# A two-layer decode step on one core: the loads of K and V regrouped, the held matrices chosen one by one, and the steps between the layers rewritten

## The chip, the cores and the metric

The kernel runs on one core of a Trainium2 chip. The metric is the device time of one execution in microseconds; the median of several executions is compared. The core has five instruction streams: TensorE (PE: matrix multiplications, with the weight loads shown apart as PEld), VectorE (DVE), ScalarE (ACT), GpSimd (POOL) and SyncE (SP), which here does little but issue transfers from device memory to on-chip memory. ACT issues some transfers too. The streams wait for each other through semaphores. The transfers themselves are carried out by 16 DMA engines.

## The reference: what is computed

Four sequences (tokens 0 to 3), each with one new vector `x` of 448 numbers, pass twice through the same attention block and the same feed-forward block. The second pass uses the same weights and the same K and V as the first, so each matrix is wanted twice.

```python
W = min(4096, max(256, Sk // 4))                     # Sk = 8192, so 2048 keys
q = (x @ wq) in 16 heads of 256
k = repeat(k_cache[:, :, Sk - W:, :], 2)             # 8 KV heads, two query heads each
v = repeat(v_cache[:, :, Sk - W:, :], 2)
o = softmax(q k^T / 16) v
attention(x) = o @ wo                                # wq 448 x 4096, wo 4096 x 448
ffn(x) = (silu(x @ w_gate) * (x @ w_up)) @ w_down    # 448 x 1792, 448 x 1792, 1792 x 448

x = x + attention(layernorm(x));  x = x + ffn(layernorm(x))    # first layer
x = x + attention(layernorm(x));  x = x + ffn(layernorm(x))    # second layer, same arguments
```

All arguments are bfloat16. For one token and one KV head, K and V are 2048 x 256 numbers each, 1 MB each. There are 4 x 8 such pairs, and each is wanted in both layers: 64 MB of K and 64 MB of V if nothing were kept (MB is 1,048,576 bytes when a matrix is meant; in sums of traffic it is a million bytes).

## The kernel before

**Names.** A matrix is written as token, layer, KV head: `K204` is the K of token 2, KV head 4, read for its first layer (0); `V2130` is the first half of the V of token 2, head 3, in its second layer (1).

**Memory.** On chip there are 27 slots of half a megabyte (`half`, `NPOOL` = 27), 4 KB on each of 128 partitions. A K or V takes two. `wq` has a place of its own, as large as seven slots. `wo`, the gate, up and down weights have theirs. Each weight is read once.

**What is kept.** The last `KEEP_K[t]` K and `KEEP_V[t]` V of token t in its first layer stay in their slots until the second layer (line 36): 21 K and 18 V in all, always whole matrices. The others are read again.

**Order of the work.** `PLAN` (line 39) lists 44 stages. A stage has one or two batches, a batch one or two pairs of K and V (`+` or `&` joins two). First come mostly token 0's first layer, then token 1's first layer with token 0's second between it, and so on. The order of every engine's operations is written out by hand: `SEQ_PE`, `SEQ_DVE`, `SEQ_ACT`, `SEQ_POOL`, `SEQ_SP` hold the numbers of the operations in the order in which `build` makes them; in `SEQ_PE` a `w` is a filler, a 128 x 512 multiplication by zeros (line 1274) that keeps TensorE busy. `SLOTS` says which slot each load takes, in SP's order. `schedule` (line 230) adds the waits: a load into a slot waits until the PE instruction that last reads the slot's old content has run. Of the first loads, those before the first that must wait for a slot, every second one is issued by ACT instead of SP. All engines work strictly through their lists, so a load that waits holds back all loads behind it on SP.

**One batch** (`group`, line 816). The loads of K (line 829 whole: one transfer of 1 MB, 8 KB in one run on each partition; line 835 in halves: 4 KB runs, which skip the other half's 4 KB) and of V (line 851, always in halves: 8 keys, 4 KB, on each partition). DVE transposes each half of K in place (841). PE computes the scores (874), DVE the maximum (890), PE spreads it over the partitions (895, 898), DVE negates it (904), ACT takes the exponential (908), PE turns the weights round (921), ACT copies them out (930), PE sums them (938), DVE finishes the sums (943), PE multiplies with V (952), POOL inverts the sums (965), ACT and DVE fold the result (968, 970), PE flips it (976), DVE scales it (1006), and PE applies `wo` (1018 as columns, 1026 as rows). The scores release the slots of K, the product with V those of V. In the last stage the product with V is formed the other way round, V as the stationary operand (989).

**Between the layers.** When a token's eight heads are done, `rows` (760) brings the rows that line 1026 summed in PSUM back into a column: ACT copies them as bfloat16 (761), DVE takes the remainder (763), PE turns both (771), DVE adds (775). `residual` (778), then `norm` (530): DVE forms the weighted sum and the sum of squares (534, 537), PE spreads them (540), DVE subtracts the mean (544) and copies the two sums (546), PE and DVE prepare the last 64 of the 448 inputs (548, 551), POOL forms the inverse deviation in three steps (556, 558, 560). Then the feed-forward block, of two kinds. `ffn` (689; for tokens 0 and 3, whose weights are stationary, 56 multiplications for gate, 56 for up) works in columns: lines 720, 731, 734, 738, 748, 756. `ffn_row` (634; tokens 1 and 2, `ROWF`) works in rows 512 wide: lines 656, 662, 664, 666, 672, 684, and needs `rows` again at its end. After it come `norm` again and `qproj` (577): two strips 512 wide (594), two copies (600), two turns (610), a copy (617), a selection (625) and a copy (630). Tokens that have ended their second layer wait for the next token's feed-forward block and go through it together with that token.

**The end.** `finale` (1057) runs the last feed-forward block in columns (1117, 1128, 1149, 1152, 1157), turns all four results into rows (1172), adds the down projection in two strips of 224 (1182), copies (1188) and stores two halves of 4 x 224 (1190).

Of the kernel before, what the change touches and what calls it, by code (L numbers as in the profile page):

```python
# [5 lines left out]
ACT = mybir.ActivationFunctionType  # L6
# [7 lines left out]
B = 4  # L14
# [21 lines left out]
KEEP_K = (5, 5, 4, 7)  # L36
KEEP_V = (6, 5, 4, 3)
ROWF = (1, 2)
# [5 lines left out]
)  # L44
WHOLE = (
    "000 002 003 004 005 006 007 010 011 100 101 102 107 114 115 200 202 206"
)
SEQ_PE = (
# [294 lines left out]
def build(nc, A_x, A_k_cache, A_v_cache, A_wq, A_wo, B_x, B_w_gate, B_w_up, B_w_down, out):  # L343
# [3 lines left out]
    with ExitStack() as es:  # L347
# [58 lines left out]
        Ab = ps("A")  # L406
        Zb, Z2 = ps("Z"), ps("Z2")
        Av = Ab[:, 448:464].rearrange("p (c t) -> p c t", t=B)


        def c_ident0(e):
            e.memset(onesb[:, :], 1.0)
# [928 lines left out]
```

## Time and profile before

| | |
|---|---|
| median of 3 executions | 287.29 us (287.08 to 287.34) |
| span of the profiled execution | 290.4 us |
| busy: PE / DVE / POOL / ACT | 251.9 / 192.0 / 82.8 / 62.9 us |
| of PE's time, fillers (339) | 102.1 us |
| read from device memory | 105.48 MB |
| median time from issue to landing: V half / K half / K whole | 7.8 / 7.3 / 13.5 us |

The profiled execution is a single one and 3.1 us longer than the median. Engine times are sums over instructions that may overlap with those of other engines. In the tables of stretches, "DMA share" is the mean busy share of the 16 DMA engines (a little over 1 is possible, since packets overlap) and the last column what they moved.

### The profile page before, as it was taken

The numbers are of one execution on the slowest core, as the hardware profiler recorded it, in microseconds if no ns is written. First come the engines' busy times: TensorE is split into PE (matmuls) and PEld (weight loads), VectorE is DVE, ScalarE is ACT, GpSimd is POOL, SyncE is SP. The second block draws the span as 40 slices with busy tenths as digits, with TensorE's granted clock in tenths as the row PEclk, the third lists the DMA queues.
The fourth block names the chain that finished last, engine by engine and source line by source line (L and its number), as shares of the span: only waits on it lengthen the run. The fifth ranks groups of instructions, "written<-read, shape, count | busy, mean of one in ns | idle before, by whom it ended". The sixth has DMA issues, their size and how long they took to land.

```text
span 290.4 us, 11178 instructions
## 1 busy us (share of the span) xinstructions
PE 251.9 (87%) x4933; PEld 141.6 (49%) x4933; DVE 192.0 (66%) x594; ACT 62.9 (22%) x178; POOL 82.8 (29%) x233
## 2 busy tenths in 40 slices
PE   3989799899898999798989898988869988879976
PEld 1434344544474454354544544454536546745675
DVE  5527756547353895887867479959697679556532
ACT  0012011121202132213223122313323231223400
POOL 0071003031024224122423231605233162245231
PEclk9999889999999999999899999999999999999957
DMA  7999999999997999999999999999999999999800
GB/s 278 420 423 417 406 415 396 402 408 403 391 402 235 368 408 416 413 414 401 349 320 407 383 418 407 408 410 374 381 387 373 415 405 353 332 342 395 350 5 0
DMA packets 29192, 106.20 MB, mean 366 GB/s; under 512 B 2900, under 2 KB 7000, under 8 KB 26840
## 3 DMA queue, kind: packets, MB, share of 16 engines
q1 hardware_dynamic: 27424, 96.12, 85.3%
q10 hardware_dynamic: 1720, 9.37, 7.9%
q8 instruction: 38, 0.62, 0.9%
q14 instruction: 10, 0.08, 0.1%
HBM read 105.48 MB, written 0.00 MB: 363 GB/s over the span
## 4 chain that ended last, share of the span: by engine, by line
PE 42%; DMA 34%; DVE 16%; issue 2%; ACT 2%; SPq 2%; POOL 1%; DVEq 0%; ACTq 0%
DMA half<-in_A_k_cache_dram 29%; PE A L1274 13%; DVE half L841 10%; PE S L874 7%; PE Y L952 6%; DMA half<-in_A_v_cache_dram 5%; PE A L1026 2%; PE Z L720 2%; DVE oh L970 2%; PE Y L921 2%; PE Z L748 1%; ACT oh L968 1%; PE A L1018 1%; DVE tiny L890 1%; SPq L851 1%
## 5 line engine op out<-in xcount | busy, mean ns | idle before, releaser
L841 DVE STREAM_TRANSPOSE half<-half 128x1024 uint32<-128x1024 uint32 x86 | 105.4, 1233 | 12.2 <-DMA half<-in_A_k_cache_dram 12.1
L1274 PE MATMUL A<-identb,small 128*128 128x512 bf16 x339 | 102.1, 401 | 5.3 <-DVE A L434 4.8
L965 POOL TENSOR_TENSOR small<-small 128x2 f32<-128x2 f32 (+1 forms) x50 | 39.2, 789 | 57.3 <-DVE small L943 55.4
L952 PE MATMUL Y<-half,pT 128*4 128x256 bf16 (+1 forms) x992 | 43.3, 272 | 6.3 <-DMA half<-in_A_v_cache_dram 3.7
L874 PE MATMUL S<-half,qe 128*8 128x128 bf16 (+1 forms) x1600 | 41.6, 236 | 6.7 <-DVE half L841 2.3
L1274 PEld LDWEIGHTS A<-identb,small 128*128 128x128 bf16 x339 | 29.4, 104 | 33.1 <-issue 12.0
L874 PEld LDWEIGHTS S<-half,qe 128*8 128x8 bf16 x1600 | 28.9, 85 | 18.8 <-DVE half L841 4.5
L908 ACT ACTIVATE praw<-S,small 104x128 bf16<-104x128 f32 (+1 forms) x50 | 19.8, 397 | 82.2 <-DVE small L904 73.7
L880 POOL TENSOR_TENSOR qe<-qc,tiny 128x64 bf16<-128x64 bf16 x64 | 17.9, 293 | 51.1 <-PE S L874 37.5
L970 DVE SCALAR_TENSOR_TENSOR oh<-oh,small,Y 128x256 bf16<-128x256 bf16 x49 | 23.1, 472 | 13.4 <-ACT oh L968 12.9
L968 ACT ACTIVATE oh<-Y 128x256 bf16<-128x256 f32 x49 | 18.7, 382 | 49.0 <-PE Y L952 43.6
L952 PEld LDWEIGHTS Y<-half,pT 128*4 128x4 bf16 (+1 forms) x992 | 18.4, 83 | 17.8 <-DMA half<-in_A_v_cache_dram 5.4
L890 DVE TENSOR_REDUCE tiny<-S 104x1 bf16<-104x128 f32 (+1 forms) x50 | 15.9, 318 | 6.0 <-PE S L874 5.9
L930 ACT ACTIVATE pT<-Y 128x64 bf16<-128x64 f32 (+1 forms) x50 | 12.6, 252 | 33.0 <-PE Y L921 28.5
L1026 PE MATMUL A<-wo_sb,oT 128*4 128x448 bf16 x200 | 16.7, 352 | 1.8 <-DVE oT L1006 1.7
L556 POOL TENSOR_SCALAR st<-st 128x1 f32<-128x1 f32 x15 | 4.0, 265 | 48.0 <-DVE st L546 47.9
L904 DVE TENSOR_REDUCE small<-S 104x1 f32<-104x32 f32 x50 | 8.8, 179 | 11.8 <-PE S L898 11.4
L1212 POOL MEMSET oT<- 128x16 bf16 x40 | 4.1, 112 | 40.1 <-PE A L1026 30.5
L943 DVE TENSOR_REDUCE small<-Y 128x2 f32<-128x32 f32 (+1 forms) x50 | 9.3, 188 | 8.8 <-PE Y L938 8.5
L1006 DVE TENSOR_TENSOR oT<-Y,small 128x4 bf16<-128x4 f32 (+1 forms) x63 | 8.9, 154 | 6.8 <-PE Y L976 5.3
L976 PEld LDWEIGHTS Y<-tiny,oh 128*128 128x128 bf16 x98 | 6.7, 100 | 10.9 <-DVE oh L970 6.0
L976 PE MATMUL Y<-tiny,oh 128*128 128x2 bf16 (+1 forms) x98 | 9.7, 168 | 2.5 <-DVE oh L970 2.1
(181 smaller groups left out, 272.5 us busy)
## 6 DMA issues: line engine op xcount, KB each, us to landing
half<-in_A_v_cache_dram SPq DMA_DIRECT2D x90, 512.0 KB, 7.8
half<-in_A_k_cache_dram SPq DMA_DIRECT2D x55, 512.0 KB, 7.3
half<-in_A_k_cache_dram SPq DMA_DIRECT2D x10, 1024.0 KB, 13.5
half<-in_A_k_cache_dram ACTq DMA_DIRECT2D x5, 1024.0 KB, 23.4
wo_sb<-in_A_wo_dram SPq DMA_DIRECT2D x7, 448.0 KB, 16.0
wq_sb<-in_A_wq_dram ACTq DMA_DIRECT2D x2, 1024.0 KB, 8.8
wd_sb<-in_B_w_down_dram SPq DMA_DIRECT2D x1, 1568.0 KB, 15.6
wg_sb<-in_B_w_gate_dram SPq DMA_DIRECT2D x1, 1344.0 KB, 9.1
```

The lines of the kernel that those rows point to most:

```text
L841: return e.transpose(a, a)
L874: last = e.matmul(Sb[s_][qd:qd + 8, 0:32 * 2 * J], lhsT=qe[q_][:, P, ce, :, :].rearrange("p a n -> p (a n)"), rhs=keys(kcs[P], J * x, J, c ...
L880: g.op(POOL, "qe", lambda e, P=P, t=t, kvh=kvh: e.tensor_tensor(qe[q_][:, P, :, :, :], qc[t][:, kvh, :, :].unsqueeze(2).broadcast_to([128, ...
L890: g.op(DVE, f"max{n}", lambda e: e.tensor_reduce(pmax[s_][0:R, :], Sb[s_][0:R, 0:N], AX.X, ALU.max), r=(f"s{s_}",), w=(f"pmax{s_}",), bank ...
L908: return e.activation(praw[0:R, 0:128 * n].rearrange("p (g r l) -> p g r l", g=2 * n, l=2), Sb[s_][0:R, 0:128 * n].rearrange("p (l g r) -> ...
L952: last = e.matmul(Yb[p_][32 * gg:32 * gg + M, 256:512], lhsT=pT[pt][:, gg, 2 * a + hv, 4 * P:4 * P + M] if n == 2 else p1[:, gg % 2, 2 * a ...
L965: g.op(POOL, f"pow{n}", lambda e: e.tensor_tensor(ri[p_][:, 0:2 * n], rs[p_][:, 0:2 * n], expo[:, 1:1 + 2 * n], op=ALU.pow), r=(f"rs{p_}", ...
L968: g.op(SCA, "oh", lambda e: e.activation(oh[:, :], Yb[p_][:, 256:512], ACT.Copy), r=(f"y{p_}",), w=("oh",), bank=(f"Y{p_}",))
L970: g.op(DVE, "oho", lambda e: e.scalar_tensor_tensor(out=oh[:, :], in0=oh[:, :], scalar=lomask[:, 0:1], in1=Yb[p_][:, 256:512], op0=ALU.mul ...
L976: last = e.matmul(Yb[p_][:, 2 * n * dh:2 * n * dh + 2 * n], lhsT=oh[:, :].rearrange("p (m e) -> p e m", e=2)[:, dh, :], rhs=osel[:, 0:2 * ...
L1026: last = e.matmul(Ab[32 * k:32 * k + B, 0:D], lhsT=oT[oi][:, k % 2, k // 2, :], rhs=wo_sb[:, 4 * kvh + k, :], start=False, stop=False, ski ...
L1274: return e.matmul(Ab[:, 0:512], lhsT=zero[:, 0:1].broadcast_to([128, 128]), rhs=identb[:, :].unsqueeze(1).broadcast_to([128, 4, 128]), sta ...
```

## The change

The plan of the 44 stages, the slots (27), and what is computed stay. What changes:

- **Loads of K and V.** V is split like K, 16 keys in one run on each partition. 27 K (before 15) and 28 V (before none) are read as one transfer of 1 MB with 8 KB runs; 34 halves of K (56) and 39 halves of V (92) remain. Counted from `PLAN`, the lists of held and of whole matrices, K and V together need 91.5 MB of 1,048,576 bytes, before 89.
- **Held matrices.** `KEEP_K` and `KEEP_V` name them: the same K but for that of token 3, head 6 (20); 33 halves of V instead of 36 (four halves are no longer kept, one is new).
- **Slots.** `wq` lies behind the 27 slots in the same tensor. Its seven slots are used for loads after the last use of `wq` (the last q projection).
- **Orders.** `SEQ_*` and `SLOTS` are new. There are 201 fillers instead of 339: before the sixth stage's scores 8 instead of 125; in the last five stages 13, before none. At the start, loads of K and V stand before `x` and between the parts of `wq`.
- **`norm`**: the sum comes as a by-product of the residual's addition, POOL has one step (`power`) instead of three and a scaling; two small DVE steps are new.
- **`rows`**: one copy as float32 and a turn with float32 weights, no remainder.
- **Feed-forward block**: gate and up for all tokens as row strips of 256, 29 multiplications each; then 128 x 256 steps on ACT and DVE, two turns, a copy, the down projection in columns.
- **Softmax weights**: the exponentials stay in plain column order; the turn takes 16 or 32 small multiplications instead of 8.
- **q**: one strip of 256 (64 multiplications in four groups), one copy, 32 small turns, one copy.
- **The end**: gate and up as strips, down in four strips of 112; two finished tokens are stored earlier, two stages before the end, the other two at the end, each token by one transfer.

```diff
-KEEP_K = (5, 5, 4, 7)
-KEEP_V = (6, 5, 4, 3)
-ROWF = (1, 2)
+KEEP_K = (
+    "03 06 01 04 07 16 14 15 13 17 23 27 26 25 33 37 31 34 35 30"
+)
+KEEP_V = (
+    "030 031 060 061 010 011 050 051 040 041 070 071 160 161 140 141 150 151 130 170 171 230 270 271 260 261 251 331 "
+    "370 310 311 340 341"
+)
+EARLY = 2
...
+        held = [None] * npool + [late] * 7
...
-        wq_sb = sb("wq_sb", [128, 3 * 4096 + 2048], BF16)
-        kv = sb("half", [128, NPOOL * HALF], BF16)
+        kv = sb("half", [128, (NPOOL + 7) * HALF], BF16)
+        wq_sb = kv[:, NPOOL * HALF:(NPOOL + 7) * HALF]
...
-                    vsrc = A_v_cache[t, kvh, s0:s0 + WIN, :].rearrange("(a q g) d -> a q (g d)", a=2, q=128)
...
+                    vsrc = A_v_cache[t, kvh, s0:s0 + WIN, :].rearrange("(p j) d -> p (j d)", p=128)
+                    whole = f"{t}{layer}{kvh}" in WHOLE_V.split()
+                    if whole:
+                        g.dma(1 << 20, lambda e, vs=vs, vsrc=vsrc: e.dma_start(
+                            kv[:, HALF * vs[0][0]:HALF * vs[0][0] + 2 * HALF], vsrc[:, :]), None,
+                            w=tuple(f"v{t}_{kvh}_{hv}" for hv in range(2)), cells=tuple(vs), run=8192)
...
+        def power(dst, key, src, n):
+            g.op(POOL, f"pr{n}", lambda e: e.tensor_tensor(dst, src[:, 0:n], expo[:, 0:n], op=ALU.pow),
+                 r=("mixf" if src is mixf else "mixq", "expo"), w=(key,))
...
+                            for c, b, o, m in parts:
+                                last = e.matmul(zb[32 * j:32 * j + 8, o:o + m], lhsT=win(b, i, 8), rhs=w[:, c:c + m],
+                                                start=(cc == 0 and i == 0), stop=False, skip_group_check=True)
...
+            g.op(SCA, "rowcp", lambda e: e.activation(wide[:, 0:D], Ab[:, 0:D], ACT.Copy), r=(f"row{t}",), w=WIDE + ("wt", "wx", "wy"), bank=("A",))
...
+                    last = e.matmul(Zb[0:m, cc:cc + 1], lhsT=wide[:, 128 * cc:128 * cc + m], rhs=nmk[:, t, 0:1],
+                                    start=False, stop=False, skip_group_check=True)
```

More of the change, by code (lines that the diff above doesn't have):

```diff
@@ L228, in _count, with schedule @@
         o.dval = self.dcount[sem]
-    def schedule(self, npool, filler):
+    def schedule(self, npool, filler, lastq):
         real = len(self.ops)
@@ L248, in schedule @@
         last = {id(c): o for o in self.ops[:real] for c in o.rel}
-        held = [None] * npool
+        late = []
+        last[id(late)] = lastq
+        held = [None] * npool + [late] * 7
         slots = iter(SLOTS.split())
@@ L278, in schedule @@
                 o.start, o.pos = t, at[e]
-                o.end = free[e] = t + DUR[o.kind]
+                o.end = free[e] = t + DUR.get(o.kind, .3)
                 if o.nbytes:
@@ L370, in build @@
-        ri = [small[:, 14 + 2 * NS + 4 * (NY + i):18 + 2 * NS + 4 * (NY + i)] for i in range(NY)]
-        fars = small[:, 11:14].bitcast(BF16)
+        tiny = sb("tiny", [128, 12 + NS], BF16)
+        onesb, qmask, osel = tiny[:, 0:1], tiny[:, 2:6], tiny[:, 6:10]
+        par = tiny[:, 10:12]
+        pmax = [tiny[:, 12 + s:13 + s] for s in range(NS)]
+        sel2 = sb("sel2", [128, 4, 2, 12], BF16)
+        sel1 = sb("sel1", [128, 4, 4, 2, 2], BF16)
+        small = sb("small", [128, 32 + 2 * NS + 8 * NY], FP32)
@@ new lines, in build @@
+        inv, lomask, expo = small[:, 0:1], small[:, 1:2], small[:, 2:7]
+        fars = small[:, 7:10].bitcast(BF16)
+        zero = small[:, 10:11].bitcast(BF16)
+        base = small[:, 11:13]
+        mixf, mixq = small[:, 13:15], small[:, 15:17]
+        ratef, rateq = small[:, 17:19], small[:, 19:20]
+        nmk = small[:, 20:28].rearrange("p (t k) -> p t k", k=2)
+        negm = [small[:, 28 + 2 * i:30 + 2 * i] for i in range(NS)]
+        rs = [small[:, 28 + 2 * NS + 4 * i:32 + 2 * NS + 4 * i] for i in range(NY)]
@@ new lines, in q_rest, with turn @@
+        def q_rest(ts):
+            n = len(ts)
+            g.op(SCA, "qcp", lambda e: e.activation(qrow, Zb[:, 0:256], ACT.Copy, scale=rateq[:, 0:1]), r=("z", "rq"),
+                 w=("wb",), bank=("Z",))
+            def turn(e):
+                last = None
+                for ce in range(8):
+                    w = qrow[:, 64 * (ce // 2):64 * (ce // 2) + 64].rearrange("p (s v) -> p v s", v=2)[:, ce % 2, :]
+                    for a in range(4):
+                        o = Z2[32 * a:32 * a + 32, 0:128 * n].rearrange("p (t x) -> p x t", t=n)
+                        last = e.matmul(o[:, 16 * ce:16 * ce + 16, :], lhsT=w, rhs=slots(ts, 4), start=(ce == 0), stop=False,
@@ L679, in down @@
             def down(e):
+                fresh(e, Zb[:, 0:4 * n])
                 last = None
-                for c in range(4):
-                    for j in range(4):
-                        if 4 * j + c < NFC:
-                            last = e.matmul(Ab[32 * j:32 * j + B, 0:D], lhsT=hT[:, 16 * c + 4 * j:16 * c + 4 * j + 4],
-                                            rhs=wd_sb[:, 4 * j + c, :], start=False, stop=False, skip_group_check=True)
-                return last
-            g.op(PE, "downr", down, r=("wb", "wd"), acc=tuple(f"row{t}" for t in ts), bank=("A",))
@@ L797, in build @@
+        for t in range(B):
+            norm(t, xs, f"xs{t}", mixq, base if t == 0 else mixq, BZ2)
+            extra(t, BZ2)
+        power(rateq[:, 0:1], "rq", mixq, 1)
+        q_part(list(range(B)), 0, 3, "qmm3")
+        q_part(list(range(B)), 3, 4, "qmm1")
+        q_rest(list(range(B)))
         seq = [p for s in plan() for b in s for p in b]
-        first = [[h for t_, layer_, h in seq if (t_, layer_) == (t, 0)] for t in range(B)]
         assert len(seq) == 2 * B * HKV and len(set(seq)) == len(seq)
@@ L1175, in rowx, with store @@
                 return x
-            g.op(PE, "xrow", rowx, r=("xh", "xl", "identb"), w=("ra",), bank=(rk,))
-            def down(e, fs):
+            g.op(PE, kind, rowx, r=("wx", "wy", "identb"), w=(key,), bank=(rk,))
+        def store(ts, engines):
+            for u, eng in zip(ts, engines):
+                o = g.dma(1000, lambda e, u=u: e.dma_start(
+                    out[u, 0, :].rearrange("(i n) -> i n", i=4), xio[u:96 + B:32, 0:W]), f"o{u}", r=xio_k, w=(f"out{u}",))
+                o.eng = eng
@@ L1199, in build @@
             where = {}
+            if si == len(PLAN) - EARLY:
+                g.tag = ("e",)
+                early([u for u in range(B) if done.get((u, 1)) == HKV and u not in waiting], gi)
+                g.tag = None
             for batch, split in zip(heads, splits):
```

735 lines of the change are left out of this document (296 added, 439 removed), and 155 rows, old and new, of tables (SEQ_ACT, SEQ_DVE, SEQ_PE, SEQ_POOL).

## The prediction

> **What bounds the kernel now.** I read the page first, then the busy time by stretches.
>
> ```profile
> span 290.4 us, 11178 instructions
> DMA packets 29192, 106.20 MB, mean 366 GB/s; under 512 B 2900, under 2 KB 7000, under 8 KB 26840
> PE 42%; DMA 34%; DVE 16%; issue 2%; ACT 2%; SPq 2%; POOL 1%; DVEq 0%; ACTq 0%
> ```
>
> ```profile
> core 0: us, PE busy (x) PEld busy (x) DVE busy (x) ACT busy (x) POOL busy (x), PEclk, DMA share, GB/s
> 10.00:20.00 10.00, 8.67 (x46) 3.93 (x44) 3.38 (x25) 0.00 (x0) 4.87 (x16) 1.00 1.01 421
> 0.00:80.00 80.00, 68.21 (x872) 32.43 (x873) 46.02 (x163) 10.81 (x32) 14.74 (x44) 0.98 1.00 396
> 80.00:100.00 20.00, 18.66 (x416) 11.43 (x415) 11.87 (x39) 3.42 (x11) 6.44 (x19) 1.00 0.90 328
> 100.00:140.00 40.00, 35.73 (x710) 18.65 (x707) 31.62 (x77) 9.61 (x29) 10.58 (x27) 0.97 1.02 408
> 140.00:160.00 20.00, 17.39 (x315) 9.00 (x313) 15.26 (x42) 6.24 (x15) 7.71 (x24) 0.98 0.95 358
> 160.00:200.00 40.00, 35.78 (x747) 19.71 (x747) 29.78 (x78) 9.46 (x27) 13.37 (x37) 1.00 1.02 403
> 200.00:220.00 20.00, 15.78 (x389) 8.83 (x377) 16.43 (x47) 6.35 (x16) 6.08 (x19) 1.00 0.99 377
> 220.00:240.00 20.00, 17.86 (x403) 10.54 (x399) 14.02 (x47) 5.73 (x18) 7.52 (x19) 1.00 1.02 406
> 240.00:260.00 20.00, 17.06 (x486) 11.99 (x487) 12.91 (x47) 4.69 (x14) 6.54 (x21) 1.00 0.96 339
> 260.00:277.00 17.00, 15.52 (x388) 9.94 (x376) 10.64 (x40) 6.00 (x16) 6.90 (x15) 1.00 0.88 348
> 277.00:290.00 13.00, 9.94 (x251) 9.12 (x251) 3.49 (x24) 0.55 (x2) 2.88 (x9) 0.61 0.01 3
> ```
>
> The last two columns decide. Up to about 275 us the transfers run nearly always: 403 to 408 GB/s at a share of 1.02 where nothing disturbs them. In four stretches they sag: 80 to 100, 140 to 160, 200 to 220 and 240 to 260 us. Against 404 GB/s the last three lose (404 - 358)/404 x 20 = 2.3, 1.3 and 3.2 us. The first carries short runs of the feed-forward weights, so I go by its share: (1.02 - 0.90)/1.02 x 20 = 2.4 us. Together 9.2 us, and after the transfers some 13 us in which nearly nothing moves. PE's 42% of the chain contains fillers; it isn't the limit where the share is 1.02.
>
> What makes them sag? The waits of SP's own queue:
>
> ```profile
> SPq L851 <- PE Y L952: 35.3, 18, 8.4
> SPq L851 <- PE S L874: 35.0, 9, 17.0
> SPq L835 <- PE Y L952: 28.3, 14, 5.2
> ```
>
> Loads wait for slots. Such a wait is harmless while enough is queued ahead of the load, so I counted that from the code. For each load that waits I took its place in SP's order, in bytes, and the end of the last load that the releasing PE instruction, or anything before it in PE's order, needs. The difference is the load's lead: what DMA can still move while the releasing work runs. At 404 GB/s a lead of 2.7 MB is 6.7 us, and 2.1 MB (two K or V) is 5.2 us. Bytes become times by the rows above (31.7 MB by 80 us, 38.2 by 100, 54.6 by 140, 61.7 by 160, 77.8 by 200, 85.4 by 220, 93.5 by 240). Loads with a lead of 2.7 MB or less, before: 7 of 12 in the first sagging stretch, 1 of 27 in the sound one behind it, then 7 of 14 (sags), 4 of 30 (sound), 8 of 14 (sags), 1 of 16 (sound), 10 of 22 (sags). The stretches that sag are those with the short leads, four times out of four. That is my reason for taking slots and their order, not the amount of arithmetic, as what costs the 9.2 us.
>
> **The change part by part.** *Traffic.* K and V go from 89 to 91.5 matrices of 1,048,576 bytes: +2.62 MB. Matrices read whole, in 8 KB runs, go from 15 to 55; 2.5 of the 40 are the additional ones, so 37.5 (39.3 MB) move from 4 KB to 8 KB runs. For 4 KB runs I take 404 GB/s, from the row 160:200. For 8 KB runs the row 10:20, in which mostly `wq` and whole K land, has 421, but with the engines nearly idle; the row 100:140 with some whole K has 408. Those are the ends; I take 417, nearer the first, which is nearly pure. Additional bytes: 2.62/0.417 = +6.3 us. Longer runs: 39.3/0.404 - 39.3/0.417 = 97.3 - 94.2 = -3.1 us. Net +3.2, between +2.3 (421) and +5.5 (408).
>
> The Trainium skill ("DMA: Bandwidth & Descriptors", section "Why small descriptors are slow (HBM only)") gives a fixed cost of about 3 cycles of 32 bytes for each packet. As an estimate from that page, 4 KB packets would lose 2.3% and 8 KB packets 1.2%, so longer runs would bring about -1.1 us and the net would be +5.2; the rows 10:20 and 160:200 differ by 4%, which speaks for more, though the first is a quieter stretch.
>
> *Leads.* The same count after the change: short leads in the same byte ranges 6 of 11, 1 of 21, 6 of 11, then none of 41 loads between 61.7 and 93.5 MB, and 2 of 21 at the end (the seven late slots of `wq` free the last loads). By the count the third and fourth sag go, 1.3 + 3.2 us, but for a rest of 0.2 + 0.6. A load of 1 MB waits for the later of two slots, and all loads behind it on SP wait too; that is in the count. The first two keep their short leads. There the releasing work contains a token's way from its last head to the next layer's first scores (tokens 0 and 1), and that becomes shorter:
>
> ```profile
> 86.12 1.79 PE Z L748 x56
> ...
> 92.44 1.27 ACT wide L600 x2
> ...
> 95.56 0.56 PE S L874 x32
> ```
>
> ```profile
> L763 DVE TENSOR_TENSOR wide<-A,wide 128x448 bf16<-128x448 f32 x11 | 6.8, 623 | 2.4 <-ACT wide L761 2.4
> L560 POOL TENSOR_TENSOR st<-st,small 128x1 f32<-128x1 f32 x15 | 8.6, 574 | 0.9
> L558 POOL TENSOR_SCALAR st<-st 128x1 f32<-128x1 f32 x15 | 4.4, 297 | 0.5
> L556 POOL TENSOR_SCALAR st<-st 128x1 f32<-128x1 f32 x15 | 4.0, 265 | 48.0 <-DVE st L546 47.9
> L540 PEld LDWEIGHTS Z<-st,small 128*128 128x128 f32 x30 | 6.1, 231 | 3.6 <-DVE st L537 2.0 <-issue 0.7 <-DVE st L551 0.4
> L664 DVE SCALAR_TENSOR_TENSOR wide<-wide,Z 128x512 f32<-128x512 f32 x2 | 1.3, 668 | 0.0
> L666 DVE SCALAR_TENSOR_TENSOR wide<-wide,small,Z 128x512 bf16<-128x512 f32 x2 | 1.5, 747 | 0.1
> L534 DVE SCALAR_TENSOR_TENSOR st<-xr,small 128x4 f32<-128x4 f32 x11 | 1.8, 160 | 0.2
> ```
>
> From the down projection (86.12) to the first scores of token 0's second layer (95.56) it takes 9.4 us. Of that go: two of three POOL steps (0.27 + 0.30), the second of the two copies (half of 1.27 = 0.6), and the steps of the lines 534, 546, 565, 617 and 625 (by the row of 534 some 0.2 each, together about 1.0); the two new DVE steps and the longer turn give back about 0.7. Net -1.5. Ahead of it gate and up: 112 multiplications at a pitch of 1.79/56 = 0.032 us are 3.6 us, 58 strips of 256 at 0.98/32 = 0.031 (the row 272.75, below) are 1.8, so -1.8. Against that ACT and DVE work on 128 x 256 instead of 128 x 14: half of 0.67 and of 0.75 plus a turn, about +1.0. `rows` loses line 763 (-0.6) and gets float32 weights: four turns, each of two passes whose weights take 0.23 us (line 540), 1.8 at most in place of eight short ones: +1.1. A token's way thus becomes about 1.8 us shorter, between 1 and 4; part of the fillers on it go too. Each of the first two sags is about 2.3 us, so I leave 0.9 and 1.1 of them. Left of 9.2 us: 0.9 + 1.1 + 0.2 + 0.6 = 2.8; saved 6.4, between 3 (only the last two, not fully) and 9.2.
>
> *Start.* The first part of `wq` now lies behind K and V on both queues, so the first scores come later, by my estimate 6 us (3 to 10). The first waiting load stands at 19.6 MB, nearly 50 us at the rate of the first row of 80 us, and until 80 us DVE is busy 46 of 80 us. I cost it at nothing; the cover is that idle time, and without it up to 6 us of sag would be added.
>
> *The end.* After the last load:
>
> ```profile
> 272.75 0.98 PE Y L952 x32
> ...
> 277.81 0.72 PE Y L989 x21
> ...
> 281.63 0.93 PE Z L1117 x28
> ...
> 285.89 2.17 PE Y L1182 x28
> 288.08 0.38 DVE wo_sb L1188
> ```
>
> The last V is now one load of 1 MB, so 32 multiplications instead of 16 wait for it (+0.5), and the turn of `rows` between them has float32 weights (+1.0). Gate, up and the strips with their longer ACT and DVE steps come out at -0.6. The down projection, 28 multiplications in 2.17 us at a clock of 0.61, becomes 56 of half the width with fillers ahead: -0.5. Sum +0.4, between -1.0 and +2.0. The early store lies behind all loads on SP, so it holds up nothing; its two POOL steps and the turn delay PE by some tenths while V is still landing. Fillers, the row steps of the other tokens and the softmax's turn cost nothing: DMA covers them; where the share is below 1, they are in the rest of 2.8 us.
>
> Sum against the profiled execution: 290.4 + 3.2 - 6.4 + 0.4 = 287.6 us. It was 3.1 us longer than the median, which I take as the same afterwards: 287.3 - 2.8 = 284.5 us.
>
> **The rivals.** *The bytes decide (slower).* If the sags belong to something that stays (the plan's stages, the same in both, with DVE 12 to 16 of 20 us busy in them), the shorter leads were a sign and not the cause. Then 2.62 MB more on a kernel that is bound by transfers remain: 287.3 + 3.2 + 0.4 = 290.9. It decides as soon as less than 3.6 us of sag go. Against it: the sound stretch 100:140 has as much DVE work (31.62 of 40).
>
> *All sags go, and 8 KB runs reach 421.* 287.3 + 2.3 - 9.2 - 1.0 = 279.4. For it: the leads at the end are 4.3 MB on average after 3.3. Against it: two groups of short leads stay.
>
> *The clock (slower).* 138 fillers go. In the row 277:290, where no filler stands, the clock is 0.61. If it falls to half in the stretches with few fillers, PE becomes the bound at the end: in 260:277 PE is busy 15.52 of 17 us, without any filler, and at half clock its blocks of 32 wide multiplications (0.98 us) would double. Some five of them on the path: +4.5, so 289.0. Against it: that stretch ran at 1.00, because it was busy.
>
> The Trainium skill states such a rule ("TensorE: Matmul & The Clock Gate", Part 1): half rate after an idle window of about 3.4 us, full rate after a busy one. The rows 260:277 and 277:290 agree with it.
>
> *No change*: half of the sag goes, 4.6 - 0.4 - 3.2 = 1.0 us at most, and a somewhat worse start or end takes it: 287.3.
>
> **How the numbers follow.** Forecast 0.60 (its own range 281.5 to 287), all sags gone 0.15, no change 0.05, the bytes 0.13, the clock 0.07. So faster by over 0.2% (0.6 us, about what a measurement can tell here) 0.75, same 0.05, slower 0.20. The range reaches down to the second rival and up beyond the clock's 289.0, and leaves out the bytes and the tail below: 279.3 to 289.5.
>
> **What would show it.** Right: HBM read 108.1 MB; the stretches that held 200:220 and 240:260 at 400 GB/s or more, those at 80:100 and 140:160 still lowest; sound stretches at 410 to 417; SP's waits shorter; first scores about 6 us later than before; the last load to the end about 13 us. Wrong: sags of the same depth at the same bytes (the count of leads was no cause), sound stretches still at 404 (runs bring nothing), PEclk near 0.5 between 100 and 270 us, or an end longer than 15 us.

## The result and the profile after

The changed kernel takes 333.92 us (331.76 to 336.68), the kernel before on the same chip 287.31 us. The ratio is 1.1634, with a 95% interval of 1.1560 to 1.1708: some 47 us slower, where 2.8 us faster was forecast. (Executions that the chip disturbed are left out of all ratios here; where too few remain for an interval, single undisturbed executions are named.) The profiled execution of the changed kernel is its fastest, that of the kernel before stood 3.1 us above its median, so the two spans differ by 39.5 us only.

From the page of the changed kernel: its span, the granted clock by fortieths of the span, the transfers, what was read, and the chain that ended last.

```profile
span 329.9 us, 12739 instructions
PEclk9999976989969999999799999877997769595998
DMA packets 24174, 108.93 MB, mean 330 GB/s; under 512 B 2356, under 2 KB 6456, under 8 KB 16696
HBM read 108.11 MB, written 0.00 MB: 328 GB/s over the span
PE 60%; DMA 15%; DVE 12%; issue 6%; ACT 4%; ACTq 1%; POOL 1%; DVEq 0%
```

The bytes are the forecast ones, and there are fewer packets than before. What changed is the chain: DMA's 34% became 15%, PE's 42% became 60%, and "issue", time in which an engine waits for nothing that the profile shows, went from 2% to 6%. TensorE, which had the largest share already, now holds most of the chain. Some stretches of the changed kernel:

```profile
core 0: us, PE busy (x) PEld busy (x) DVE busy (x) ACT busy (x) POOL busy (x), PEclk, DMA share, GB/s
0.00:80.00 80.00, 35.86 (x773) 20.68 (x777) 46.31 (x150) 8.45 (x26) 9.48 (x29) 0.91 0.96 382
90.00:100.00 10.00, 10.00 (x162) 6.94 (x161) 1.36 (x12) 0.22 (x1) 1.52 (x4) 0.66 0.44 147
100.00:110.00 10.00, 8.82 (x231) 4.39 (x223) 7.42 (x17) 2.26 (x7) 3.30 (x10) 1.00 0.87 303
110.00:140.00 30.00, 26.80 (x658) 13.16 (x654) 22.81 (x55) 7.04 (x23) 8.22 (x22) 1.00 1.02 417
140.00:170.00 30.00, 26.54 (x586) 17.55 (x585) 17.85 (x55) 5.51 (x17) 6.51 (x16) 0.94 0.92 334
170.00:210.00 40.00, 34.83 (x799) 19.80 (x793) 28.04 (x68) 8.60 (x25) 11.19 (x29) 1.00 1.02 410
210.00:240.00 30.00, 27.28 (x600) 16.73 (x596) 15.82 (x50) 5.00 (x15) 5.25 (x15) 0.83 0.84 318
260.00:270.00 10.00, 10.00 (x146) 6.03 (x146) 4.27 (x15) 1.75 (x6) 0.70 (x1) 0.50 0.48 180
280.00:290.00 10.00, 9.38 (x184) 6.06 (x187) 3.56 (x18) 1.23 (x4) 2.21 (x7) 0.66 0.58 213
311.00:330.00 19.00, 15.09 (x377) 10.46 (x376) 5.14 (x28) 2.43 (x6) 3.17 (x6) 0.91 0.01 3
```

Stretches without a sag reach 417 and 410 GB/s, as predicted. But the sags are deeper than before: 147, 180 and 213 GB/s, and in those rows PE is busy 9.4 to 10.0 of 10 us. In SP's own queue the loads still wait, and for the same two kinds of work, scores and the product with V, now for up to 21 us:

```profile
SPq L784 <- PE Y L883: 39.6, 10, 11.3
SPq L756 <- PE S L808: 27.3, 6, 21.1
SPq L756 <- PE Y L883: 20.6, 7, 5.0
```

A load that waits for a slot shows only that PE is late. To see where PE got late I took for each of the 50 batches the start of its maximum on DVE, after minus before. Eleven of them, named by the batch, and the end of the span:

| batch | 000 (first) | 004 | 101 (11th) | 013 | 200 | 110+203 | 213 (36th) | 215 | 210 | 313+317 | 316&310 (last) | end |
|---|---|---|---|---|---|---|---|---|---|---|---|---|
| later by, us | 17.1 | 11.6 | 5.2 | 7.3 | 9.4 | 11.6 | 19.5 | 22.8 | 28.1 | 30.1 | 36.8 | 39.5 |

A bad start is mostly caught up by the eleventh batch; then some 34 us are lost. The loss isn't even: 9 us up to the 35th batch (14.3 us late, at 206 us of the kernel before), and 25 us in the last 84 us.

### The profile page after: what moved, and what is told of

It reads as the page before. It is cut to its first block, busy times and chain, and to the rows that moved or that the text cites. A ratio compares the mean times of both kernels' runs of the same rounds, so it can differ in the third digit from the quotient of the medians.

```text
span 329.9 us, 12739 instructions
## 1 busy us (share of the span) xinstructions
PE 257.4 (78%) x5770; PEld 156.8 (48%) x5770; DVE 189.1 (57%) x570; ACT 55.6 (17%) x168; POOL 66.4 (20%) x176
## 3 DMA queue, kind: packets, MB, share of 16 engines
HBM read 108.11 MB, written 0.00 MB: 328 GB/s over the span
## 4 chain that ended last, share of the span: by engine, by line
PE 60%; DMA 15%; DVE 12%; issue 6%; ACT 4%; ACTq 1%; POOL 1%; DVEq 0%
PE A L1170 11%; PE S L808 10%; DMA half<-in_A_wq_dram 10%; PE Y L883 9%; DVE half L768 6%; DMA half<-in_A_v_cache_dram 6%; PE Z L662 5%; PE Z L582 4%; PE Z L626 3%; PE A L952 3%; PE Y L852 3%; PE Z L688 2%; PE A L944 2%; DVE oh L899 1%; PE Y L905 1%
## 5 line engine op out<-in xcount | busy, mean ns | idle before, releaser
L1170 PE MATMUL A<-identb,small 128*128 128x512 bf16 x201 | 71.5, 420 | 0.5 <-DVE xr L698 0.3
L808 PE MATMUL S<-half,qe 128*8 128x128 bf16 (+1 forms) x1600 | 47.0, 250 | 13.5 <-issue 8.2
L883 PE MATMUL Y<-half,pT 128*4 128x256 bf16 (+1 forms) x992 | 49.6, 300 | 2.7 <-issue 1.1
L808 PEld LDWEIGHTS S<-half,qe 128*8 128x8 bf16 x1600 | 32.0, 89 | 23.5 <-issue 11.4
L883 PEld LDWEIGHTS Y<-half,pT 128*4 128x4 bf16 (+1 forms) x992 | 18.9, 86 | 17.4 <-issue 9.2
L563 POOL TENSOR_TENSOR small<-small 128x1 f32<-128x1 f32 (+1 forms) x10 | 6.3, 628 | 100.9 <-DVE small L550 81.4
L814 POOL TENSOR_TENSOR qe<-qc,tiny 128x64 bf16<-128x64 bf16 x64 | 18.0, 294 | 42.0 <-PE S L808 27.9
L1170 PEld LDWEIGHTS A<-identb,small 128*128 128x128 bf16 x201 | 17.1, 104 | 15.9 <-issue 10.1
L852 PE MATMUL Y<-sel,praw 104*32 104x16 bf16 (+1 forms) x1024 | 15.9, 175 | 7.2 <-ACT praw L842 3.9
L852 PEld LDWEIGHTS Y<-sel,praw 104*32 104x32 bf16 x1024 | 12.1, 96 | 15.4 <-issue 6.6
L875 DVE TENSOR_REDUCE small<-Y 128x2 f32<-128x32 f32 (+1 forms) x50 | 9.4, 190 | 15.8 <-PE Y L871 12.7
L419 PE MATMUL Z<-identb,small 128*128 128x4 bf16 (+2 forms) x13 | 2.3, 177 | 18.3 <-DMA wo_sb<-in_A_x_dram 18.0
L662 PE MATMUL Z<-wide,wd_sb 128*128 128x1 bf16 (+1 forms) x224 | 16.2, 175 | 0.0
```

Of the source, the lines that this page charges most:

```text
L662: last = e.matmul(Zb[0:m, n * cc:n * cc + n], lhsT=wd_sb[:, f, 128 * cc:128 * cc + m], rhs=hT[:, n * f:n * f + n], start=False, stop=False ...
L808: last = e.matmul(Sb[s_][qd:qd + 8, 0:32 * 2 * J], lhsT=qe[q_][:, P, ce, :, :].rearrange("p a n -> p (a n)"), rhs=keys(kcs[P], J * x, J, c ...
L814: g.op(POOL, "qe", lambda e, P=P, t=t, kvh=kvh: e.tensor_tensor(qe[q_][:, P, :, :, :], qc[t][:, kvh, :, :].unsqueeze(2).broadcast_to([128, ...
L852: last = e.matmul(Yb[p_][32 * a:32 * a + 32, C * k:C * k + C], lhsT=praw[0:R, 32 * k:32 * k + 32], rhs=w, start=(k == 0), stop=False, skip ...
L883: last = e.matmul(Yb[p_][32 * (j % 4):32 * (j % 4) + M, 256:512], lhsT=pcol(P, hv, j, M, 4 * P), rhs=unit(vss[P][hv])[:, 256 * j:256 * j + ...
L1170: return e.matmul(Ab[:, 0:512], lhsT=zero[:, 0:1].broadcast_to([128, 128]), rhs=identb[:, :].unsqueeze(1).broadcast_to([128, 4, 128]), sta ...
```

## The experiments

Five theories were on the table, the first three from the beginning, the others formed after the first results. (1) The clock: fewer fillers, so TensorE at half rate; by the granted clock TensorE ran at half rate for 65 us of the changed kernel's span and for 17 us of the other's. (2) The start. (3) Single steps on a token's way that became longer, the down projection above all. (4) The turn of the softmax weights in 16 or 32 small multiplications: PE's instructions don't arrive in time. (5) PE's in-order list has become full altogether, so that each thing on it costs time, fillers too; sags, waits and late slots only follow.

Effects below are differences of ratios times 287.3 us, against the changed kernel's 1.1634. "Fillers" are the 128 x 512 multiplications by zeros.

**Clock: more and fewer fillers.** The orders get 102 more `w` at 24 places (e1), or every second `w` goes (e4 in the kernel before, 170 of 339 left; e7 in the changed kernel, 101 of 201 left).

> The kernel after with 102 more fillers (303 in place of 201), put into the stretches ahead of which its clock falls to half; nothing else changes. Theory 1, the clock: TensorE runs at half rate for about 65 of 330 us, because the multiplications of 3.4 us use too little of the array, and work at half rate is what makes loads wait. Then the half-rate time shrinks to 25 us or less and the time falls from 333.9 to between 305 and 322 us; the fillers themselves cost up to 20 us of TensorE time, partly where it waits. Theory 2, the late start: x and wq land behind K and V, and nothing later makes up for it. Then at most 5 us are gained. Theory 3, longer steps between the layers (down projection 3.9 in place of 1.8 us, turns with float32 weights): more fillers on that way make it slower, 335 to 345 us.

> The kernel before with every second filler taken out (170 of 339 left), nothing else. Theory 1, the clock: half-rate periods appear between 40 and 270 us, 40 us of them or more, and the time rises from 287.3 to between 300 and 320 us. Theories 2 and 3: fillers do nothing that the result needs, and TensorE has 50 us less to do; 285 to 288 us.

> The kernel after with every second filler taken out (101 of 201 left). With 102 more fillers it became 9 us slower although the clock rose from 0.90 to 0.945. Theory 5, TensorE's own list is what is late: the fillers stand on it, 100 fewer save 10 to 25 us at a given clock, and the clock falls to 0.80 to 0.87; together 325 to 332 us. Theory 1, the clock: 340 to 355 us.

With 303 fillers the granted clock rose from 0.90 to 0.95, half-rate time fell from 65 to 37.5 us, and the time did not fall: 343.06 us median, 335.47 us in the one undisturbed execution. With 101 the clock fell to 0.84, and the kernel became 6.3 us faster (1.1414 [1.1325, 1.1503]). The kernel before with half its fillers took 288.4 us, at a clock of 0.89, in its one undisturbed execution, 293.56 us in the median. Each of these edits changes the clock and the length of PE's list at once, and shows only the sum of the two. In the changed kernel a filler costs more by its place on the list than it brings by the clock, so the 47 us can't be bought back with fillers; what the clock costs by itself isn't shown.

**The start.** In e3 SP issues `x` and the parts of `wq` ahead of K and V (the first four slots are exchanged to match):

```diff
-    "97 235 90 118 41 93 44 40 211 237 188 43 115 165 168 139 42 215 ..."
+    "44 40 41 118 42 43 93 97 235 90 211 237 188 115 165 168 139 215 ..."
```

In e5, besides, the ten K transposes that stand between the steps of the first norms in DVE's order move behind them; in e18, besides, the first token's q is copied ahead of six of them.

> The kernel after with the first issues in another order: the short part of wq, x and the other three parts of wq go first, K of the first two pairs between them; all later loads and all slots stay. Theory 2, the start: first scores at about 30 us in place of 44.8, and 10 to 17 us gained, 317 to 324 us. Theory 1, the clock: the 17 us were mostly caught up by the third stage (delay 6 to 7 us until the first boundary), so 3 to 7 us gained, 327 to 331 us. Theory 3, the steps: as theory 1.

> The kernel after with the order of issues of the run before last (short part of wq, x and the other parts of wq first) and, in addition, VectorE's order: the first ten transposes of K stand behind the norm of the four tokens in place of between its steps. Theory 2a, VectorE's own order made the start late (its norm steps stood behind transposes that waited for K until 17, 23 and 28 us): first scores at 24 to 30 us in place of 44.8, and of the 17 us the 5 to 7 us stay gained that were not caught up by the eleventh stage: 326 to 330 us. Rival: the first multiplications wait for slots and weights anyway, under 2 us gained, 332 to 335 us.

> The kernel after with both orders of the run e5 and, in addition, the cast of the first token's q ahead of six of the ten transposes (in e5 the first scores came at 36.5 us in place of 44.8, because that cast stood behind all ten and ran at 35.6). The first scores now come at 24 to 30 us. If the late start is passed on to the end, 10 us or more are gained against the kernel after: ratio to before 1.12 or less. If the held-up work is caught up while transfers fill the slots, as the stages' times say (the delay fell from 17 to 6 us by the eleventh stage without any edit), no more than in e5: ratio 1.125 to 1.145.

e3 brought nothing that its interval shows (1.1576 [1.1371, 1.1780]): `x` arrived at 7.2 us instead of 18, but the first scores came at 47.3. The order of DVE was the reason, as its first work in the changed kernel shows (the number in brackets is the idle time ahead; in e3 the first transpose starts at 17.24 us): it waits for K, transposes it, and the steps of the norm stand between further transposes, which start at 18.9, 23.3, 27.9, 32.8, 35.5 and 37.9 us. The copy of q and the first maximum follow.

```profile
17.30 1.25 DVE L768 STREAM_TRANSPOSE half<-half 128x1024 uint32<-128x1024 uint32 x1 [14.41 <-DMA half<-in_A_k_cache_dram]
18.47 0.13 DVE L499 TENSOR_REDUCE tiny<-identb 128x2 bf16<-128x16 bf16 x1
...
27.94 3.46 DVE L768 STREAM_TRANSPOSE half<-half 128x1024 uint32<-128x1024 uint32 x3
...
43.80 0.29 DVE L605 CAST qc<-Z 128x128 bf16<-128x128 f32 x1 [4.27 <-PE Z L600]
45.83 0.29 DVE L824 TENSOR_REDUCE tiny<-S 104x1 bf16<-104x128 f32 x1 [1.73 <-PE S L808]
```

In e5 the copy of q still stood behind the transposes, at 35.59 us, and the first scores came at 36.5 us; the kernel gained 9.1 us with a wide interval (1.1316 [1.1154, 1.1478]). e18 had the first scores at 24.7 us, but their maximum waited on DVE until 36 us again, and it gained 7.0 us (1.1390 [1.1329, 1.1452]). The start is worth about 7 us of the 47.

**The down projection.** The changed kernel alternates between 128 and 64 weight columns: the fourth column block has only 64. e17 exchanges the two loops; e2 also makes each multiplication 32 columns wide by repeating the operand.

```diff
-                for f in range(NFC):
-                    for cc in range(4):
+                for cc in range(4):
+                    for f in range(NFC):
```

> The kernel after with the down projection's loops turned round (the same 128 or 64 columns of weights 14 times running) and its moving operand repeated to 32 columns, as before the change. Theory 1, the clock: besides 2.1 us saved in each of four down projections (8 us), the half-rate periods that follow them (92.6, 157.5, 225.7, 280.4 us: together 20 us) go; 10 to 18 us gained, 316 to 324 us. Theory 2, the start: under 3 us. Theory 3, the steps: 4 x 2.1 = 8 us, half rate stays; 325 to 327 us.

> The kernel after with the loops of the down projection turned round and nothing else: one or two moving columns stay, but 14 multiplications running have the same 128 (or 64) columns of weights. If the change of width between neighbours makes a multiplication take 70 ns in place of 33, the block of 56 falls from 3.9 to 1.8 to 2.0 us and the time to 324 to 328 us, as with 32 columns. If it is the one or two moving columns, the block stays at 3.9 us and the time at 332 to 336 us.

The same block of 56 multiplications, first in the changed kernel, then in e17:

```profile
89.52 4.07 PE L662 MATMUL Z<-wide,wd_sb 128*128 128x1 bf16 x56
```

```profile
87.97 1.72 PE L662 MATMUL Z<-wide,wd_sb 128*128 128x1 bf16 x56
```

The order alone is worth 2.35 us a block and 10.5 us in all (e17 1.1270 [1.1190, 1.1351]); the wider operand adds nothing (e2 1.1324 [1.1153, 1.1495], 8.9 us). The starts of the 56 in the changed kernel's trace tell what costs it: they are 25 ns apart between neighbours of 128 columns, although the output column changes there too, 93 ns to the one of 64 and 123 ns back. So it is the change of width, 28 times a block, 84 ns each on average.

**The rows.** e8 copies a finished row as bfloat16 and turns it in four multiplications, as the kernel before does, without its remainder.

> The kernel after with the copy and the turn of rows in bfloat16, without the remainder that the kernel before added (so the sums of wo lose some digits): 8 turns of 4 multiplications. Theory 3, steps between the layers: the turn takes 0.15 to 0.3 us in place of 0.88 (1.58 at half rate), 8 times on a token's way: 5 to 8 us gained, 326 to 329 us. Rival, the way is hidden: under 2 us.

The turn in the changed kernel, then in e8:

```profile
81.57 1.01 PE L688 MATMUL Z<-small,wide 128*128 128x1 f32 x8
```

```profile
82.75 0.33 PE L689 MATMUL Z<-small,wide 128*128 128x1 bf16 x4
```

In the kernel before, with its remainder:

```profile
278.39 0.35 PE L771 MATMUL Z<-tiny,wide 128*128 128x1 bf16 x8
```

e8 gained 8.9 us (1.1325 [1.1230, 1.1421]). It leaves out the remainder, so part of that isn't the number format's.

**The softmax's turn: instructions or time?** e6 puts the turn of the changed kernel into the kernel before: each multiplication becomes four.

```diff
-                        last = e.matmul(Yb[p_][64 * h:64 * h + 64, c0:c0 + (48 if n == 2 else 32)],
-                                        lhsT=praw[0:R, 64 * gg:64 * gg + 64], rhs=w, ...
+                        C = 24 if n == 2 else 16
+                        for u in range(2):
+                            for v in range(2):
+                                last = e.matmul(Yb[p_][64 * h + 32 * u:64 * h + 32 * u + 32, c0 + C * v:c0 + C * v + C],
+                                                lhsT=praw[0:R, 64 * gg + 32 * u:64 * gg + 32 * u + 32],
+                                                rhs=w[:, C * v:C * v + C], ...
```

e9 puts time on PE's list of the kernel before without many instructions: 124 fillers behind the turns, some 26 us. e13 makes the changed kernel's turn with a quarter of the multiplications; three quarters of what the turn computes are left out.

> The kernel before with one part of the change alone: the softmax's turn takes 1024 multiplications of 32 columns of weights by 16 or 24 in place of 256 of 64 by 32 or 48; all else stays. Theory 4, instructions: TensorE has 1536 more of them (6 packets of 16 KB) and runs dry while the next packet is on its way. Then gaps without a wait, which end 1.2 to 1.5 us behind such a packet, appear (5 to 12 of them, one before), and the time rises by 6 to 20 us. Theory 3, longer steps alone: 24 more multiplications at 0.031 us in 50 batches are 0.75 us each, mostly where transfers are the bound; 0 to 5 us, no gaps.

> The kernel before with 124 more fillers, two or four right behind each of the softmax's turns: about 124 x 0.21 = 26 us more work for TensorE at the places where the small turns added 768 x 0.031 = 24 us, but 248 instructions in place of 1536. Theory 4, instructions: the small turns cost 13.7 us because their instructions don't arrive in time; the fillers then cost 0 to 6 us and leave 0 to 2 gaps without a wait. Theory 5, TensorE's list: its time alone counts, so 11 to 17 us, 299 to 306 us, without such gaps.

> The kernel after with the softmax's turn in 256 multiplications, as many as before, in place of 1024: one for each group of keys, with 128 columns of weights and the first of the four selectors alone; the other three quarters of the softmax's weights are left out (replaced by wrong ones). Theory 5, TensorE's list: 768 x 0.031 = 24 us less of TensorE's time; as the small turns cost the kernel before 13.7 us, 12 to 20 us gained, 314 to 322 us. Rival, the small turns matter only where transfers set the pace: under 6 us gained.

e6 made the kernel before 13.9 us slower (1.0485 [1.0363, 1.0606]). My expectation priced each small multiplication at 0.031 us, 24 us in all. That was wrong: the block of 32 in e6 takes 0.38 us where 8 took 0.31 before (the first line), and over 50 batches PE's time for the turns grew only from 12.9 to 16.7 us. What cost more is seen in the brackets of e6's timeline, gaps in which PE waited for nothing that the trace names, in the middle of a block:

```profile
105.39 0.31 PE L921 MATMUL Y<-selt,praw 104*64 104x48 bf16 x8
```

```profile
104.58 0.38 PE L924 MATMUL Y<-selt,praw 104*32 104x24 bf16 x32
...
107.37 0.26 PE L924 MATMUL Y<-selt,praw 104*32 104x24 bf16 x11
108.75 0.30 PE L924 MATMUL Y<-selt,praw 104*32 104x24 bf16 x19 [1.12 <-issue]
...
114.94 0.39 PE L956 MATMUL Y<-half,pT 128*8 128x256 bf16 x7 [1.41 <-issue]
```

e6 has 11 such gaps, 10.8 us; the kernel before has one of 1.2 us. (Both, and e9, have one more at 17.8 us, ahead of the first q projection; it is of another kind, as shown below.) Added: 3.8 + 9.6 = 13.4 us, near the measured 13.9; that all of it reaches the end is assumed. e9, with none of these gaps and one instruction packet more than before, became 15.7 us slower (1.0548 [1.0463, 1.0634]), at a clock of 0.98. PE's list had no 26 us to spare, not even where the transfers had run at a share of 1.02: the two sound stretches of the prediction's table, 408 and 403 GB/s there, are in e9

```profile
100.00:140.00 40.00, 38.08 (x708) 18.84 (x709) 30.46 (x66) 9.00 (x28) 10.61 (x29) 1.00 0.99 395
160.00:200.00 40.00, 37.78 (x700) 19.44 (x699) 28.63 (x71) 9.51 (x27) 12.75 (x35) 1.00 1.00 393
```

The chain of e9, then of e6:

```profile
PE 70%; DVE 12%; DMA 9%; ACT 3%; issue 2%; POOL 2%; SPq 1%; DVEq 0%; ACTq 0%
```

```profile
PE 63%; DVE 16%; DMA 8%; issue 7%; ACT 3%; POOL 2%; SPq 0%; POOLq 0%; DVEq 0%; ACTq 0%
```

Both turned a kernel with PE at 42% into one with PE at 63% or more; the change makes it 60%. In e13, 313.08 us in its one undisturbed execution and 319.34 in the median, 15 to 21 us came back, with less work done, and 4.4 us of gaps stayed of 13.3.

**Why PE waits for nothing.** A gap of the same kind in the changed kernel's timeline, 24 of 32 multiplications of one block ahead of it and 8 behind, and another:

```profile
68.15 0.54 PE L808 MATMUL S<-half,qe 128*8 128x128 bf16 x24 [0.57 <-POOL qe L814]
70.77 0.29 PE L808 MATMUL S<-half,qe 128*8 128x128 bf16 x8 [2.08 <-issue]
...
299.27 1.88 PE L808 MATMUL S<-half,qe 128*8 128x256 bf16 x32 [3.49 <-issue]
```

In the list of queues, the transfers of kind "instruction" (packets, MB, share) are these, for the changed kernel, the kernel before and e6:

```profile
q8 instruction: 45, 0.74, 0.9%
```

```profile
q8 instruction: 38, 0.62, 0.9%
```

```profile
q8 instruction: 44, 0.72, 0.9%
```

They are packets of 0.74/45 MB, 16 KB. One is under way from 68.2 to 69.3 us, the next gap's from 297.0 to 298.0. Each of the changed kernel's 12 gaps over 0.3 us ends 1.2 to 1.6 us after such a packet has landed. And if PE's records are counted from the start of the trace (multiplications, weight loads and its sequencer's), the record that ends a gap always has 193 or 194 more than a multiple of 256 ahead of it: 705, 962 and 1218 for the first three, 10433 for the last. The same holds for all 167 such gaps of the twenty traces; only the one at 17.8 us in the kernel before, e4, e6 and e9 is otherwise (62 or 88 records and no packet ahead of it). So PE had run out of instructions, at the end of a block of 256, and waited for the next 16 KB. The Trainium skill ("Runtime: NRT & Kernel Launch", section "Instruction fetch mechanics") says that instructions come in blocks of 16 KB, 256 instructions, and that the crossing is mostly hidden. The size agrees; at 33 of the changed kernel's 45 boundaries there is no gap over 0.3 us, at the other 12 the crossing costs 13.3 us. That these packets lie in DMA's queues behind loads is likely: over all traces the next packet starts 9.7 us (median) after PE has crossed a boundary where DMA's share is 0.95 or more, and 6.5 us where it is under 0.2. But PE's own pace differs between the two as well, so no run shows it.

**Together.** e10 joins e2, e5 and e8; e14 adds e13's turn, with what that leaves out; e11 is e10 with every second filler gone, e16 with 102 more.

> The kernel after with three of the edits above together: down projection wide and in the other order, rows in bfloat16 without remainder, and both orders of the start. If what they save lies on one list that is late (theory 5), it adds up: 8 + 6 + 3 = 17 us, 314 to 320 us. If they share what they save (each only shortens the same wait for transfers), 320 to 326 us. In both cases at least 25 us more than before remain, since the small turns stay (13.7 us by themselves).

> The same with every second filler taken out (101 of 201 left). Theory 5, TensorE's list: 100 fillers fewer are 21 us less of TensorE's time; the kernel after gained 3.5 us by it, at a clock that fell from 0.90 to 0.84. Here 2 to 8 us less than the run with three edits, 308 to 316 us. Theory 1, the clock: 5 us or more longer.

> The three edits together (313.1 us) and, in addition, the turn in 256 multiplications, three quarters of its work left out. Theory 5: another 10 to 16 us gained, 297 to 303 us. What then remains against before (8 to 14 us) is traffic (+3.2 us by the prediction's sum), the rest of the start (2 to 4 us) and the end. Rival, something of the change that was not tried yet (strips of gate, up and q; the order of the loads) carries the most: 305 us or more.

> The three edits together (313.1 us) with 102 more fillers at the places of the first run (303 in place of 201). Half the fillers cost this version 6 us, at a clock that fell from 0.91 to 0.85; in the kernel after, 102 more cost 9 us at a clock that rose from 0.90 to 0.945. Theory 5, TensorE's list: 102 x 0.21 = 22 us more of its time, partly paid back by the clock: 314 to 322 us. Theory 1, the clock, which would now show because the list is less late: 302 to 309 us.

| kernel | median us | ratio | against the changed kernel |
|---|---|---|---|
| e10 | 313.14 | 1.0851 [1.0763, 1.0938] | -22.5 us; the single edits sum to -26.9 |
| e11, half the fillers | 319.12 | 1.1051 [1.0938, 1.1163] | +5.7 on e10, clock 0.85 |
| e16, 102 fillers more | 321.84 | 1.1229 [1.1129, 1.1328] | +10.9 on e10, clock 0.94 |
| e14 | 305.33; 302.39 and 303.34 undisturbed | | -31; 15 to 18 us above the kernel before |

With three edits undone, fewer fillers cost time again and more of them too: of the three numbers tried, 201 is the best. In e14, with no filler more, the half-rate time is 27.6 us in place of 65 and the clock 0.95, so much of the lost clock followed from the four steps themselves. The chain of e14 comes near the shares of the kernel before:

```profile
PE 47%; DMA 24%; DVE 15%; issue 4%; SPq 4%; ACT 3%; POOL 1%; DVEq 0%
```

No version tried beats the kernel before.

Compared batch by batch in the profiled executions, which are 11 us apart, e14 starts 9 us late, is level with the kernel before (within 2.2 us) from the 11th batch to the 35th, that is up to 206 us, and loses 9 us from there to the last batch and 11 us to the end. So what the four edits don't bring back lies in the last third.

**Long runs.** e12 (on the changed kernel) and e15 (on e14) issue each load of 1 MB as two of half a megabyte, in 4 KB runs, with the same slots and waits.

```diff
 ...
-                            kv[:, HALF * vs[0][0]:HALF * vs[0][0] + 2 * HALF], vsrc[:, :]), None,
+                            kv[:, HALF * (vs[0][0] + i):HALF * (vs[0][0] + i) + HALF], vsrc[:, HALF * i:HALF * i + HALF])
+                            for i in range(2)], None,
 ...
```

> The kernel after with each load of 1 MB issued as two transfers of half a megabyte in runs of 4 KB, with the same waits and slots. The longer runs' term: the sound stretches fall from 415 to 422 GB/s back to 402 to 408, but TensorE sets the pace, so the time changes by 0 to 3 us: 333 to 338 us. Rival, transfers of 1 MB land late and hold up the work: two halves land earlier or more evenly, 325 to 331 us.

> The four edits together, and each load of 1 MB issued as two transfers of half a megabyte in runs of 4 KB. If transfers set the pace again by then, the longer runs' term of the prediction (3.1 us) shows: 2 to 4 us longer than the run with four edits; the sound stretches fall from about 417 to about 405 GB/s. If TensorE still sets it: within 1 us.

Where PE is the limit the longer runs bring nothing: e12, without them, has 1.1477 [1.1379, 1.1575]. On e14 they do, 306.79 and 308.65 us undisturbed without them, 4.8 us more. Two sound stretches of e14, then of e15:

```profile
110.00:140.00 30.00, 26.90 (x555) 13.66 (x557) 25.11 (x62) 6.38 (x21) 8.38 (x23) 1.00 1.02 414
170.00:210.00 40.00, 35.63 (x716) 20.75 (x719) 27.68 (x72) 7.98 (x24) 9.97 (x26) 0.91 1.00 404
```

```profile
110.00:140.00 30.00, 26.55 (x533) 13.76 (x521) 24.17 (x58) 6.38 (x21) 8.03 (x23) 0.96 1.03 407
170.00:210.00 40.00, 34.95 (x698) 19.80 (x699) 27.91 (x71) 7.98 (x24) 10.66 (x27) 0.91 1.02 395
```

## Why the prediction was wrong

**The step that failed** is the pair of sentences "it isn't the limit where the share is 1.02" and "Fillers, the row steps of the other tokens and the softmax's turn cost nothing: DMA covers them". DMA was the limit of the kernel before by little only: 26 us more on PE's list in e9 cost 15.7 and took the sound stretches from a share of 1.02 to 1.00. PE was busy 251.9 of 290.4 us; of that, 102.1 us were fillers, which I took for idle time. But a filler stands in the order, and what is behind it waits. The change put more on the list than there was room for. It has 71.5 us of fillers, 30.6 less, and still PE's busy time rose to 257.4 us, so all other work on it grew by some 36 us. (An estimate of the clock's part in that: PE was busy 60 us at half rate, before 16; 32 score multiplications of 256 columns take 1.88 us there, in the line at 299.27, and 1.05 at full rate in the kernel before. That makes some 20 of the 36.) Undone one by one, the steps gave back: the turns about 14 us (e6; by e13, which does less work, 15 to 21), the order of the down projection 10.5, the float32 turn of the rows 8.9, and the start, which lies in DVE's order and not on PE's list, 7.0. That is 40 of 47 us; undone together, 31, since they overlap. The rows that could have warned were in the prediction: in its sound stretches PE was busy 35.7 and 35.8 of 40 us, and the chain gave PE the largest share. Its table also has a fifth sagging stretch, 260:277 at 348 GB/s, which its 9.2 us leave out.

**Traffic, +3.2.** Bytes and rates were right: 108.11 MB against 108.1, sound stretches at 417 and 410. The longer runs bring 1.7% and 2.3% (e14 against e15), less than the 3.2% that I took from the nearly idle row, more than the 1.1% that I estimated from the Trainium skill's page ("DMA: Bandwidth & Descriptors", section "Why small descriptors are slow (HBM only)"), 2.3 less 1.2. What the additional bytes cost in time wasn't measured alone.

**Leads, -6.4.** Wrong. A lead in bytes tells what a wait may cost if the releasing work keeps its pace. PE's work did not: the waits for it got up to 21 us long, and the later stretches, in which the sags were to go, lost most, 25 of 34 us.

**A token's way, -1.8.** Wrong in sign. From the copy of the rows to the copy of q it took 18.8, 24.4, 25.5 and 21.7 us for the four tokens before and 20.8, 24.7, 27.7 and 31.2 after, 14 us more in all. Gate and up came out as computed, 58 strips in 2.1 us against 1.8. The down projection, which I left at its 1.79 us although its order and width change, took 4.07. The turn of the rows took 1.01 in place of 0.35, less than the +1.1 that I had allowed.

**Start, nothing.** Wrong. Not 6 but 16.7 us until the first scores, and about 7 us of it reach the end. I had counted only the transfers' order, not the norm steps behind DVE's transposes.

**The end, +0.4.** Wrong: from the landing of the last load to the end it is 19.9 us, before 12.7: +7.2. It stayed in e10 (20.7 us) and is 16.5 us in e14.

**Rivals.** None held as it stands. "The bytes decide" and "the clock" had the sign right, with 290.9 and 289.0 us. Transfers were no longer the limit: e12 gives up the longer runs without loss. The clock's condition did come, 0.50 in 260:270 and 0.66 in 90:100, and its part is larger than the +4.5 us of that rival if the estimate above holds (20 us at e9's price are some 12); but fillers that raise the clock don't bring the time down (e1). "PE's list is full" was not among the rivals. Three of the prediction's own signs of being wrong came: sags that didn't shrink, a clock near 0.5 between 100 and 270 us, an end longer than 15 us.

**Open** are the last 15 to 18 us between e14 and the kernel before: 3.2 of them fit the traffic and 3.8 the end. The rest may lie in the strips of q, gate and up, in the new orders and slots or in the held matrices, which weren't tried apart; by the batches most of it arises after 206 us. Open is also what the clock costs by itself.

## What to carry to other kernels

An engine that works strictly through a list is as full as the list, fillers included: before costing an added step at nothing, ask how much later the list can run before the slots it frees are late, and measure it by putting harmless time on it. Count instructions as well as time, since many tiny multiplications can outrun the supply of instructions; a gap that waits for nothing, in the middle of a block, is its mark. A wait for a slot names the engine that frees it, so look at that engine before counting bytes.

## What the runs showed of the hardware

Half-rate time comes in pieces of 3.4 us and its multiples (3.41, 6.83 and 10.24). Ahead of 4 of the changed kernel's 11 pieces PE is counted busy for all of 3.41 us; all four follow or overlap the down projection in its alternating order. Ahead of the piece at 277.2 us of the kernel before it is busy 2.58 of 3.40 us. The Trainium skill ("TensorE: Matmul & The Clock Gate", Part 1) speaks of an idle window of about 3.4 us: the length agrees, "idle" doesn't by the profile's count, so the prediction's word that the rows 260:277 and 277:290 agree with it holds for the direction only. The windows ahead of the eleven hold mostly multiplications with 4 to 32 weight columns or one to four moving columns, and at most three fillers, so being busy with little of the array may count as idle; no run tests that by itself.

PE's instructions arrive in blocks of 256, and PE can outrun them: 12 gaps, 13.3 us, in the changed kernel, each at the end of a block. 32 multiplications of 32 weight columns took 0.38 us where 8 of 64 columns took 0.31: small ones cost little time, only their instructions do. And a change between 128 and 64 weight columns costs 84 ns on average in the down projection.
